# Column-tiled projections, spread Wo rows and DMA-transposed inputs in a recurrent attention kernel

## The chip, the cores and the metric

The kernel runs on one core of a Trainium2 chip. The metric is the device time of one execution in microseconds (us). A kernel's time is the median of its runs.

Names: PE is TensorE (PEld its weight loads), DVE is VectorE, ACT is ScalarE, POOL is GpSimd, SP is the engine that issues the DMAs.

## The reference, cut to what matters

```python
# S = 2048 rows, D = 512, 32 heads of 128, segments of 32 rows, 8 memory rows
mem = mem0
for s in range(64):                                # one segment after another
    h = concat([mem, x_ln[:, 32*s:32*s+32]])       # 8 memory rows + 32 rows of x
    q, k, v = h @ Wq, h @ Wk, h @ Wv               # 512 -> 32 heads x 128
    p = softmax(mask(q @ k.T * scale))
    o = (p @ v) @ Wo                               # 4096 -> 512
    mem = o[:, :8]                                 # goes into the next segment
    outs.append(o[:, 8:])
h = x + concat(outs)
# ... then a gMLP over h: gelu(LN(h) @ w_in), a 2048x2048 mix, w_out ...
```

The memory makes the 64 segments a chain. Of each segment's rows, 32 (8 memory rows and the first 24 rows of x) go through the chain. The last 8 rows of x are projected ahead, for 16 segments at once: that is the "X work" below. It does not depend on the chain, so the kernel uses it to fill PE's waits.

## The kernel before

A recorder collects operations for each engine, works out the semaphore waits, and emits everything unrolled. `pe(...)`, `dve(...)`, `act(...)`, `pool(...)`, `sp(...)` record one operation for that engine, and each engine runs its own in the recorded order.

The X work for Q and K: one 128x128 stationary block for each head and quarter of D, with 128 columns moving. One group is four heads, 16 matmuls:

```python
    def qkx_mm(ck, i, bank, hhs=range(4)):
        mi, h0 = i // 8, 4 * (i % 8)
        ws = (w_q, w_k)[mi]
        for hh in hhs:
            h = h0 + hh
            for dc in range(DC):                       # DC = 4
                pe(lambda e, h=h, dc=dc, hh=hh: e.matmul(ps[:, bank, hh * 128:(hh + 1) * 128],
                       lhsT=ws[:, dc, h * DH:(h + 1) * DH], rhs=hTe[:, ck % 3, dc, :],
                       start=(dc == 0), stop=(dc == DC - 1)), ...)
```

The chain's own projections, the Wo rows and the X work for V use four column tiles of 32: `tile_position=(0, 32 * c)`, output to 32 partitions. PV uses row tiles (`tile_position=(32 * c, 0)`). PV is the product p @ v, and its result is the context. Wo in the step is the context times Wo. F_group and WoX_scatter gather the finished output rows of a row block. An evacuation is a copy out of PSUM, where the matmuls write. One step, cut:

```python
    for s in range(NSEG):                              # NSEG = 64
        j4, rb = s % 4, s // 4                         # four steps are one row block of 128 rows
        # ... QK projections, mem_out(s - 1, 1), then `late` of the step before ...
        # ... S, exp, V, sums, ln, normalise (cut) ...
        xs = gx.pop(0) if gx else []                   # a V group in steps 0-15, a Q/K group in 16-47
        late = []
        for f in xs[:2]:                               # half of the X group
            f()
        PV_half(s, 0)
        PV_half(s, 1)
        for f in xs[2:4]:                              # the other half
            f()
        if j4 == 3 and rb > 0:
            F_group(rb - 1, WXB)
            WoX_scatter(rb - 1, WXB)
        # ... six context evacuations on ACT and DVE (cut) ...
        if j4 == 3 and rb > 0:
            F_add(rb - 1, WXB)
        Wo(WOQ, OB, 0, OC)
        # ... rest of Wo, part_evac, mem_out(s, 0): the memory rows for the next step (cut) ...
        if j4 == 3 and rb > 0:
            late.append(lambda rb=rb: h_done(rb - 1))
        late += xs[4:]                                 # the X group's evacuation, on DVE
        if j4 == 1 and 2 <= rb + 2 < RB:
            ln_inplace(0)                              # layernorm of a later x block, on DVE
        if j4 == 2 and 2 <= rb + 2 < RB:
            xT(0, FBK)                                 # four PE transposes
            late.append(lambda rb=rb: ring_copy(rb + 2, FBK))   # ACT
        if s + 1 < NSEG and s >= 3:
            WoX_mm((s + 1) // 4 - 1, (j4 + 1) % 4)     # batched Wo rows: 8 matmuls of 512 columns
        # ... loads, the evacuation of the Wo rows and the first steps' own cases (cut) ...
```

Of the kernel before, what the change touches and what calls it, by code (L numbers as in the profile page):

```python
# [169 lines left out]
def fast_path(nc, st, keep, A_x, A_mem0, A_Wq, A_Wk, A_Wv, A_Wo, A_seg_len, B_w_in, B_w_sp, B_b_sp, B_w_out, out):  # L170
# [82 lines left out]
    vext_d = nc.dram_tensor("vext_d", [NCK, 128, H * DH], BF, kind="Internal").ap()  # L253
    xn2_d = nc.dram_tensor("xn2_d", [RB, 128, D], BF, kind="Internal").ap()
    h_d = nc.dram_tensor("h_d", [RB, 128, D], BF, kind="Internal").ap()
    wT_d = nc.dram_tensor("wT_d", [S // 64, 128, RB, 64], BF, kind="Internal").ap()

    ps = st.enter_context(nc.psum_tensor("f_ps", [128, 8, 512], F32))
# [5 lines left out]
    def PB(b):  # L264
        return ("ps", b)
# [28 lines left out]
    def load_xe(ck, j):  # L294
        t, tok = xbuf(j)
        sp(lambda e: e.dma_start(t, xe[CK * ck:CK * ck + CK, XM:SEG, :]), writes=tok)
# [80 lines left out]
    def slot(s):  # L377
        return s % NSLOT

    def ring_copy(rb, bank):  # L380
        src = psb[:, bank, 0:512].rearrange("p (dc s c) -> p s dc c", dc=DC, s=4, c=SEG)[:, :, :, 0:XM]
        s0 = slot(4 * rb)
        act(lambda e: e.activation(out=hT[:, s0:s0 + 4, :, M:32], in_=src, func=ACT.Copy),
            reads=[PB(bank)], writes=[("hTx", rb % 3)])
# [14 lines left out]
# [5 lines that stand above are left out]
            for dc in range(DC):  # L404
                pe(lambda e, h=h, dc=dc, hh=hh: e.matmul(ps[:, bank, hh * 128:(hh + 1) * 128], lhsT=ws[:, dc, h * DH:(h + 1) * DH],  # L405
                                                         rhs=hTe[:, ck % 3, dc, :], start=(dc == 0), stop=(dc == DC - 1)),
                   reads=[("hTe", ck % 3), ("W", mi, h // 8)], writes=[PB(bank)])

    def qkx_evac(ck, i, bank, eng="act"):
        mi, h0 = i // 8, 4 * (i % 8)  # L410
        dst = QTx[ck % 2][:, mi, :, h0:h0 + 4, :].rearrange("p s h k -> p h s k")
        src = ps[:, bank, :].rearrange("p (h s k) -> p h s k", h=4, k=8)
        if eng == "act":
            act(lambda e: e.activation(out=dst, in_=src, func=ACT.Copy), reads=[PB(bank)], writes=[("QTx", ck % 2, mi, i % 8)])
        else:
            dve(lambda e: e.tensor_copy(out=dst, in_=src), reads=[PB(bank)], writes=[("QTx", ck % 2, mi, i % 8)])
# [76 lines left out]
    def qx_copy(s):  # L493
        j = s % CK
        buf = (s // CK) % 2
        dst = QT[:].rearrange("p b hp q r -> p (b hp) q r")[:, :, 0:8, :].rearrange("p hp q r -> p hp r q")
        src = QTx[buf][:, 0, j, :, :].rearrange("p (hp r) q -> p hp r q", r=2)
        pool(lambda e: e.tensor_copy(out=dst, in_=src), reads=[("QTx", buf, 0, i) for i in range(8)],
             writes=[("QTe", 0), ("QTe", 1)])
# [170 lines left out]
    def load_h(rb):  # L670
        sp(lambda e: e.dma_start(hbuf[:, rb % 2, :], xr[:, rb, :]), writes=[("h", rb % 2)])

    def WoX_mm(rb, qr):
        for bg in range(8):
            b, g = bg // 4, bg % 4
            h = 16 * b + 4 * qr + g
            pe(lambda e, h=h, g=g, i=8 * qr + bg: e.matmul(ps[32 * g:32 * g + 32, WXB, :], lhsT=cTx[:, rb % 2, i, :], rhs=w_o[:, h, :],  # L677
                                                           start=(i < 4), stop=(i >= H - 4), tile_position=(0, 32 * g)),
               reads=[("cTx", rb % 2), ("Wo", h // 8)], writes=[PB(WXB)])
# [4 lines left out]
    def WoX_scatter(rb, bank):  # L684
        for c in range(4):
            q = slice(32 * c, 32 * c + 32)
            pe(lambda e, q=q, c=c: e.matmul(ps[q, bank, :], lhsT=Sc[:, q], rhs=partx[:], start=False, stop=True, tile_position=(0, 32 * c)),
               reads=["partx", "Sc"], writes=[PB(bank)])
# [102 lines left out]
    gx = []  # L791

    def qkx_group(ck, i):
        gx.append([lambda hh=hh: qkx_mm(ck, i, XB, (hh,)) for hh in range(4)] + [lambda: qkx_evac(ck, i, XB, "dve")])

    def vx_group(ck, n):
        gx.append([lambda dc=dc: vx_mm(ck, n, XB, dc) for dc in range(DC)] + [lambda: vx_evac(ck, n, XB, "dve")])
# [21 lines left out]
               writes=[("wT", tb % 2, t)], after=after)  # L819

    lastop = {}
    qx_copy(0)
    for s in range(NSEG):
        j4 = s % 4
        rb = s // 4
        if j4 == 1 and rb > 0:
            load_h(rb - 1)
        if s == NSEG - 1:
            load_h(rb)
        if s % 2 == 1 and s // 2 < NWT:  # L830
            wT_piece(s // 2)
        if j4 == 0 and 2 <= rb + 2 < RB:
            load_x(rb + 2, 0)
        if s == 1:
            load_xe(3, 1)

        QK(s, QKP[0], (0, 1))
        if s > 0:
            mem_out(s - 1, 1)
            for f in late:  # L840
                f()
        QK(s, QKP[1], (0, 1))
        QK(s, QKP[0], (2, 3))
        QK_evac(QKP[0])
        QK(s, QKP[1], (2, 3))
        QK_evac(QKP[1])
        for piece in QKP[2:]:
            QK(s, piece)
            lastop["qk"[piece[3]]] = em.by_eng["pe"][-1]
            QK_evac(piece)  # L850
        if s == NSEG - 1:
            load_wT(0, [lastop["q"]])
        if s == 0:
            mask_pe()
        S_half(s, 0)
        sm_exp(0)
        V_half(s, 0, (0, 1, 2))
        sm_sums(0)
        sm_ln(0)
        S_half(s, 1)  # L860
        lastop["s"] = em.by_eng["pe"][-1]
        sm_exp(1)
        sm_rcp(0)
        V_half(s, 0, (3,))
        V_evac(0, "dve")
        if s == NSEG - 1:
            sp(lambda e: e.dma_start(w_in1, winr[:, :, 0:FH]), writes=["w_in1"], after=[lastop["s"], lastop["x"]])
            sp(lambda e: e.dma_start(bsp_b, bass.AP(B_b_sp.tensor, B_b_sp.offset, [[0, 128], [1, S]])), writes=["bsp"], after=[lastop["k"]])
            for r in range(8, RB - 2):
                xn2T_dma(r, [lastop["s"], lastop["x"]])  # L870
        V_half(s, 1, gs=(0, 2))
        sm_norm(0)
        V_evac(1, "dve", (0, 2))
        sm_sums(1)
        sm_ln(1)
        sm_rcp(1)
        V_half(s, 1, gs=(2, 4))
        lastop["v"] = em.by_eng["pe"][-1]
        V_evac(1, "act", (2, 4))
        sm_norm(1)  # L880
        if s + 1 < NSEG:
            qx_copy(s + 1)
            lastop["x"] = em.by_eng["pool"][-1]
            lastop["x"] = em.by_eng["pool"][-1]
        xs = gx.pop(0) if gx else []
        late = []
        for f in xs[:2]:
            f()
        PV_half(s, 0)
        PV_half(s, 1)  # L890
        for f in xs[2:4]:
            f()
        if j4 == 3 and rb > 0:
            F_group(rb - 1, WXB)
            WoX_scatter(rb - 1, WXB)
        cT_evac(0, "act", (0,))
        cT_evac(2, "dve", (0,))
        cT_evac(0, "act", (1,))
        cT_evac(2, "dve", (1,))
        cT_evac(1, "act")  # L900
        cT_evac(3, "dve")
        if j4 == 3 and rb > 0:
            F_add(rb - 1, WXB)
        Wo(WOQ, OB, 0, OC)
        part_evac(s, OB, 0, OC)
        Wo(WOQ[:6], OB2, OC, D)
        if s + 1 < NSEG:
            mem_out(s, 0)
            mask_dve()
        Wo(WOQ[6:], OB2, OC, D)  # L910
        cTx_copy(s)
        part_evac(s, OB2, OC, D)
        if j4 == 3 and rb > 0:
            late.append(lambda rb=rb: h_done(rb - 1))
        late += xs[4:]
        if j4 == 1 and 2 <= rb + 2 < RB:
            ln_inplace(0)
        if s == 3:
            ln_inplace(1)
        if j4 == 2 and 2 <= rb + 2 < RB:  # L920
            xT(0, FBK)
            late.append(lambda rb=rb: ring_copy(rb + 2, FBK))
        if s == 5:
            xT(1, FBK)
            late.append(lambda: xe_copy(3, FBK))
        if s + 1 < NSEG and s >= 3:
            WoX_mm((s + 1) // 4 - 1, (j4 + 1) % 4)
            if j4 == 2:
                late.append(lambda rb=rb: WoX_evac(rb - 1))
        if s + 1 == NSEG:  # L930
            for f in late:
                f()
        if s + 2 < NSEG:
            load_vx(s + 2)
        if j4 == 0 and rb >= 2:
            xn2_apply(rb - 2, rb % 2)
            xn2_store(rb - 2, rb % 2)
        if s == 3 * CK:
            free0 = [done47["s"], done47["x"]]
            sp(lambda e: e.dma_start(w_in2, winr[:, :, FH:F]), writes=["w_in2"], after=free0)  # L940
        if 0 <= s - 3 * CK - 1 < 8:
            xn2T_dma(s - 3 * CK - 1, free0)
        if s == 3 * CK - 1:
            done47 = {"s": lastop["s"], "x": px}
        px = lastop.get("x")
# [924 lines left out]
```

## Time and profile before

| | |
|---|---|
| time, median of 3 runs (4 with the one timed beside the change) | 902.19 us (902.04) |
| span of the profiled run | 903.8 us |
| to the first memory cast (prologue) | 69.3 us |
| V steps (memory casts 1 to 16) | 155.7 us |
| Q/K steps (16 to 48), 32 steps | 331.3 us, 10.35 us per step |
| last steps (48 to 63), without X work | 152.3 us |
| rest (last step, gMLP) | 195.2 us |

A step is measured from one "memory cast" to the next: the small DVE cast (128x16) that brings half of the new memory rows out of PSUM. The profile page first. Its lines are the span, PE's busy share, the busy share of 40 slices in tenths (PE, granted clock, DMA), the instruction queue (packets, MB, share), and the shares of the chain that ended last:

```profile
span 903.8 us, 48903 instructions
...
PE 870.1 (96%) x22506; PEld 537.7 (59%) x22513; DVE 499.6 (55%) x1231; ACT 451.9 (50%) x1274; POOL 156.4 (17%) x403
...
PE   7989999999999999999999999899999999999997
...
PEclk9999999999999999999999999999999999999999
DMA  9971211322203020312113120404123590022101
...
q8 instruction: 178, 2.92, 1.3%
...
PE 88%; DVE 7%; issue 2%; ACT 1%; POOL 1%; DMA 0%; SPq 0%; ACTq 0%
```

PE looks full. But matmuls overlap in these records, so "busy" says only that something was in flight.

The timeline of PE from V to Wo in a plain Q/K step (start, length, line, operation, tiles, count):

```profile
406.71 0.61 PE L573 MATMUL f_ps<-f_arena,f_hT 128*32 128x256 bf16 x16
407.26 0.62 PE L405 MATMUL f_ps<-f_hTe,f_arena 128*128 128x128 bf16 x8
407.81 0.27 PE L592 MATMUL f_ps<-f_E_sb,f_V_sb 32*128 32x40 bf16 x16
...
408.03 0.27 PE L592 MATMUL f_ps<-f_E_sb,f_V_sb 32*128 32x40 bf16 x16
...
408.34 0.62 PE L405 MATMUL f_ps<-f_hTe,f_arena 128*128 128x128 bf16 x8
408.89 0.84 PE L627 MATMUL f_ps<-f_arena,f_cT 128*32 128x256 bf16 x24
```

L573 is V, L405 the X work, L592 PV, L627 Wo. The X halves stand before and after PV, where PE would otherwise wait for the softmax and for the context evacuations. The last steps have no X work and take the same 9.95 us.

DVE at the start of a plain step, and of the step after the layernorm. The first stream transpose of Q starts 2.68 us after the memory cast of 400.76 in the first case, 3.45 us after that of 410.72 in the second, behind the layernorm (L353, L363) and the X cast (L416):

```profile
401.69 0.68 DVE L416 CAST f_arena<-f_ps 128x512 bf16<-128x512 f32 x1
403.44 0.45 DVE L491 STREAM_TRANSPOSE f_QT<-f_Tst 128x256 uint32<-128x256 uint32 x1 [1.06 <-ACT f_Tst L483]
...
411.34 0.69 DVE L353 BATCH_NORM_STATS2 f_st<-f_xn 128x6 f32<-128x512 bf16 x1
...
413.24 0.41 DVE L363 TENSOR_SCALAR f_xn<-f_xn,f_mv,f_rs 128x512 bf16<-128x512 bf16 x1 [1.00 <-POOL f_rs L357]
413.56 0.68 DVE L416 CAST f_arena<-f_ps 128x512 bf16<-128x512 f32 x1
414.17 0.43 DVE L491 STREAM_TRANSPOSE f_QT<-f_Tst 128x256 uint32<-128x256 uint32 x1
```

And the matmuls of the Q/K stage as groups (busy us, mean ns of one | idle time of PE just before them, in all):

```profile
L627 PE MATMUL f_ps<-f_arena,f_cT 128*32 128x256 bf16 x2056 | 64.8, 273 | 0.0
L405 PE MATMUL f_ps<-f_hTe,f_arena 128*128 128x128 bf16 x512 | 39.7, 221 | 0.0
```

### The profile page before, as it was taken

The numbers are of one execution on the slowest core, as the hardware profiler recorded it, in microseconds if no ns is written. First come the engines' busy times: TensorE is split into PE (matmuls) and PEld (weight loads), VectorE is DVE, ScalarE is ACT, GpSimd is POOL, SyncE is SP. The second block draws the span as 40 slices with busy tenths as digits, with TensorE's granted clock in tenths as the row PEclk, the third lists the DMA queues.
The fourth block names the chain that finished last, engine by engine and source line by source line (L and its number), as shares of the span: only waits on it lengthen the run. The fifth ranks groups of instructions, "written<-read, shape, count | busy, mean of one in ns | idle before, by whom it ended". The sixth has DMA issues, their size and how long they took to land.

```text
span 903.8 us, 48903 instructions
## 1 busy us (share of the span) xinstructions
PE 870.1 (96%) x22506; PEld 537.7 (59%) x22513; DVE 499.6 (55%) x1231; ACT 451.9 (50%) x1274; POOL 156.4 (17%) x403
## 2 busy tenths in 40 slices
PE   7989999999999999999999999899999999999997
PEld 6665666566666666666666666556566544434443
DVE  3435556566666656566666666555655554543343
ACT  2335566555566655666555666556665655300000
POOL 1501111121211211112212112111111122100000
PEclk9999999999999999999999999999999999999999
DMA  9971211322203020312113120404123590022101
GB/s 327 377 211 45 62 54 42 71 62 57 72 27 68 22 71 21 76 34 55 53 42 58 35 69 22 123 26 93 41 48 63 176 275 1 1 99 76 59 12 37
DMA packets 99586, 71.50 MB, mean 79 GB/s; under 512 B 62248, under 2 KB 84912, under 8 KB 99376
## 3 DMA queue, kind: packets, MB, share of 16 engines
q1 hardware_dynamic: 99376, 68.32, 27.6%
q8 instruction: 178, 2.92, 1.3%
q14 instruction: 32, 0.26, 0.1%
HBM read 39.46 MB, written 18.61 MB: 64 GB/s over the span
## 4 chain that ended last, share of the span: by engine, by line
PE 88%; DVE 7%; issue 2%; ACT 1%; POOL 1%; DMA 0%; SPq 0%; ACTq 0%
PE f_ps L472 21%; PE f_ps L627 13%; PE f_ps L573 11%; PE f_ps L1012 11%; PE f_ps L405 7%; PE f_ps L424 3%; PE f_ps L592 3%; PE f_ps L677 3%; PE f_ps L974 3%; PE f_ps L1005 3%; PE f_ps L1083 3%; PE f_ps L539 2%; DVE f_V_sb L584 2%; PE f_ps L598 1%; PE f_ps L519 1%
## 5 line engine op out<-in xcount | busy, mean ns | idle before, releaser
L472 PE MATMUL f_ps<-f_arena,f_hT 128*32 128x512 bf16 (+1 forms) x5120 | 239.9, 337 | 0.1
L472 PEld LDWEIGHTS f_ps<-f_arena,f_hT 128*32 128x32 bf16 x5120 | 125.8, 96 | 94.2 <-ACT f_hT L656 23.0
L483 ACT ACTIVATE f_Tst<-f_ps 128x512 bf16<-128x512 f32 (+1 forms) x320 | 148.5, 512 | 56.7 <-PE f_ps L472 47.1
L573 PE MATMUL f_ps<-f_arena,f_hT 128*32 128x256 bf16 (+1 forms) x3072 | 143.5, 308 | 0.5
L627 PE MATMUL f_ps<-f_arena,f_cT 128*32 128x256 bf16 x4096 | 133.5, 275 | 6.4 <-ACT f_cT L612 4.6
L563 POOL TENSOR_TENSOR f_E_sb<-f_R_sb,f_E_sb 128x64 bf16<-128x64 f32 x128 | 48.0, 375 | 409.3 <-ACT f_R_sb L555 409.3
L627 PEld LDWEIGHTS f_ps<-f_arena,f_cT 128*32 128x32 bf16 x4096 | 95.6, 96 | 29.2 <-ACT f_cT L612 11.5
L491 DVE STREAM_TRANSPOSE f_QT<-f_Tst 128x256 uint32<-128x256 uint32 x128 | 56.9, 445 | 89.5 <-ACT f_Tst L483 89.5
L1012 PE MATMUL f_ps<-f_arena 128*128 128x512 bf16 x448 | 103.0, 384 | 2.4 <-DVE f_arena L1018 1.6
L639 ACT ACTIVATE f_part<-f_ps 128x256 bf16<-128x256 f32 x128 | 49.0, 383 | 92.7 <-PE f_ps L627 92.7
L584 DVE TENSOR_SCALAR f_V_sb<-f_ps 128x512 bf16<-128x512 f32 (+1 forms) x128 | 70.6, 551 | 41.1 <-PE f_ps L573 41.1
L614 DVE TENSOR_SCALAR f_cT<-f_ps 128x160 bf16<-128x160 f32 (+1 forms) x192 | 61.0, 374 | 39.3 <-PE f_ps L598 39.3
L1012 PEld LDWEIGHTS f_ps<-f_arena 128*128 128x128 bf16 x448 | 43.9, 99 | 57.2 <-DVE f_arena L1018 2.6
L573 PEld LDWEIGHTS f_ps<-f_arena,f_hT 128*32 128x32 bf16 x3072 | 68.8, 96 | 14.5 <-ACT f_Tst L483 1.8
L612 ACT ACTIVATE f_cT<-f_ps 128x160 bf16<-128x160 f32 (+1 forms) x192 | 53.0, 349 | 40.0 <-PE f_ps L598 40.0
L405 PE MATMUL f_ps<-f_hTe,f_arena 128*128 128x128 bf16 x1024 | 70.4, 223 | 0.1
L491 DVE STREAM_TRANSPOSE f_KT<-f_Tst 128x128 uint32<-128x128 uint32 (+1 forms) x192 | 63.8, 338 | 3.1
L405 PEld LDWEIGHTS f_ps<-f_hTe,f_arena 128*128 128x128 bf16 x1024 | 58.9, 99 | 9.2 <-issue 7.1
L551 ACT ACTIVATE f_R_sb<-f_ps 128x160 f32<-128x160 f32 x128 | 38.8, 303 | 35.8 <-PE f_ps L544 35.8
L654 DVE CAST f_hT<-f_ps 128x16 bf16<-128x16 f32 x63 | 11.0, 175 | 78.2 <-PE f_ps L648 78.2
L1018 DVE TENSOR_TENSOR f_arena<-f_ps,f_arena 128x512 f32<-128x512 f32 x28 | 19.3, 691 | 59.5 <-PE f_ps L1012 59.5
L559 DVE TENSOR_TENSOR f_E_sb<-f_R_sb,f_E_sb 128x160 bf16<-128x160 f32 x128 | 45.6, 356 | 0.0
(103 smaller groups left out, 1089.5 us busy)
## 6 DMA issues: line engine op xcount, KB each, us to landing
wT_d<-f_wst SPq DMA_DIRECT2D x32, 256.0 KB, 2.5
f_arena<-wT_d SPq DMA_DIRECT2D x32, 256.0 KB, 4.3
f_arena<-in_A_Wq_dram SPq DMA_DIRECT2D x4, 1024.0 KB, 8.6
f_arena<-in_A_Wv_dram SPq DMA_DIRECT2D x4, 1024.0 KB, 14.3
f_arena<-in_A_Wk_dram SPq DMA_DIRECT2D x4, 1024.0 KB, 14.5
f_arena<-in_A_Wo_dram SPq DMA_DIRECT2D x4, 1024.0 KB, 8.5
f_Vx<-vext_d SPq DMA_DIRECT2D x64, 64.0 KB, 2.7
f_xn<-in_A_x_dram SPq DMA_DIRECT2D x17, 128.0 KB, 2.5
```

What stands on the lines that cost most here:

```text
L405: pe(lambda e, h=h, dc=dc, hh=hh: e.matmul(ps[:, bank, hh * 128:(hh + 1) * 128], lhsT=ws[:, dc, h * DH:(h + 1) * DH], rhs=hTe[:, ck % 3, d ...
L472: pe(lambda e, dc=dc, c=c, rhs=rhs: e.matmul(ps[32 * c:32 * c + 32, bank, 0:32 * nh], lhsT=hT[:, sl, dc, :], rhs=rhs, start=(dc == 0), sto ...
L483: act(lambda e: e.activation(out=st_.rearrange("p (hp i r) -> p hp i r", i=32, r=2), in_=ps[:, bank, 0:64 * np_].rearrange("p (hp r i) -> ...
L491: dve(lambda e: e.transpose(out=dst, in_=src), reads=tok, writes=[(nm, b, k) for k in halves(b, p0, np_)])
L563: pool(lambda e: e.tensor_tensor(out=ev, in0=rv, in1=ev, op=ALU.mult), reads=[("R", b), ("Ex", b)], writes=[("Ex", b)])
L573: pe(lambda e, dc=dc, c=c, c0=c0: e.matmul(ps[32 * c:32 * c + 32, bank, 0:w], lhsT=hT[:, sl, dc, :], rhs=w_v[:, dc, c0:c0 + w], start=(dc ...
L584: dve(lambda e: e.tensor_scalar(out=dst, in0=src, scalar1=VSC, scalar2=None, op0=ALU.mult), reads=[PB(bank)], writes=tok)
L612: act(lambda e: e.activation(out=dst, in_=src, func=ACT.Copy, scale=UNSC), reads=[PB(PVB[c])], writes=tok)
L614: dve(lambda e: e.tensor_scalar(out=dst, in0=src, scalar1=UNSC, scalar2=None, op0=ALU.mult), reads=[PB(PVB[c])], writes=tok)
L627: pe(lambda e, h=h, g=g, i=i, b=b, c=c: e.matmul(ps[32 * g:32 * g + 32, bank, 0:d1 - d0], lhsT=cTh[:, i, 8:40], rhs=w_o[:, h, d0:d1], star ...
L639: act(lambda e: e.activation(out=part[:, s % 8, d0:d1], in_=ps[:, bank, 0:d1 - d0], func=ACT.Copy), reads=[PB(bank)], writes=[("part", s % ...
L1012: pe(lambda e: e.matmul(ps[:, bank, 0:TB], lhsT=z2[:, sc, fb * 128:(fb + 1) * 128], rhs=wTb[tb % 2][:, :, sc, :], start=(sc == 0), stop=(s ...
```

## The change

Its intent: the same arithmetic in fewer PE mode changes and with less work on the chain.

- X work for Q/K in four column tiles of 32, as its neighbours V and Wo are. It can then follow V, and precede Wo, without a change of PE's tiling mode.
- Batched Wo rows in units of 4 matmuls, spread over the step's end and the wait before PV.
- x blocks transposed by DMA through a scratch tensor. Four PE transposes and an ACT copy go, and a DVE copy comes.
- DVE side work (layernorm, X evacuation) spread so that it does not delay the stream transposes.

The core of the diff:

```diff
+    def x_flip(j, i, dst, tok):
+        t, rd = xbuf(j)
+        sp(lambda e: e.dma_start(xs_d[i], t), reads=rd, writes=[("xs", i)])
+        sp(lambda e: e.dma_start_transpose(out=dst, in_=xs_d[i]), reads=[("xs", i)], writes=[tok])
...
+    def qkx_cols(ck, i, bank, hh):
+        mi, h = i // 8, 4 * (i % 8) + hh
+        ws = (w_q, w_k)[mi]
+        for dc in range(DC):
+            for c in range(4):
+                pe(lambda e, dc=dc, c=c: e.matmul(ps[32 * c:32 * c + 32, bank, hh * 128:(hh + 1) * 128],
+                                                  lhsT=ws[:, dc, h * DH + 32 * c:h * DH + 32 * c + 32], rhs=hTe[:, ck % 3, dc, :],
+                                                  start=(dc == 0), stop=(dc == DC - 1), tile_position=(0, 32 * c)),
...
     def qkx_group(ck, i):
-        gx.append([lambda hh=hh: qkx_mm(ck, i, XB, (hh,)) for hh in range(4)] + [lambda: qkx_evac(ck, i, XB, "dve")])
+        gx.append([lambda hh=hh: qkx_cols(ck, i, XB, hh) for hh in range(4)] + [lambda: qkx_evac(ck, i, XB, "dve")])
...
-        for f in xs[:2]:
-            f()
-        PV_half(s, 0)
-        PV_half(s, 1)
-        for f in xs[2:4]:
-            f()
+        nw1, nw4 = ((1, 1, 1, 0)[j4], (2, 2, 0, 1)[j4]) if s < 3 * CK else (3, 0)
         if j4 == 3 and rb > 0:
             F_group(rb - 1, WXB)
             WoX_scatter(rb - 1, WXB)
+        xs = gx.pop(0) if gx else []
+        fill = xs[:4]
+        if j4 == 3 and s < 3 * CK:
+            fill = xs[1:4]
+        for f in fill[:-2]:
+            f()
+        for f in wq[:nw1]:
+            f()
+        del wq[:nw1]
+        PV_half(s, 0)
+        PV_half(s, 1)
+        for f in fill[-2:]:
+            f()
...
+            late += xs[4:]                             # step 3 of a row block
+        else:
+            for f in xs[4:]:                           # the X evacuation, now before Wo
+                f()
...
-        if j4 == 2 and 2 <= rb + 2 < RB:
-            xT(0, FBK)
-            late.append(lambda rb=rb: ring_copy(rb + 2, FBK))
+        if j4 == 0 and 2 <= rb + 2 < RB:
+            late.append(lambda: ln_stats(0))
+        if j4 == 0 and 2 <= rb + 1 < RB:
+            late.append(lambda rb=rb: ring_fill(rb + 1))
...
+            if j4 == 3:
+                wq.extend(lambda rb=rb, k=k: WoX_mm(rb, k // 2, range(4 * (k % 2), 4 * (k % 2) + 4)) for k in range(8))
+            elif j4 == 2 and gx:
+                gx[0][0]()
+            for f in wq[:nw4]:
+                f()
```

More of the change, by code (lines that the diff above doesn't have):

```diff
@@ L255, in fast_path @@
     h_d = nc.dram_tensor("h_d", [RB, 128, D], BF, kind="Internal").ap()
+    xs_d = nc.dram_tensor("xs_d", [RB + 1, 128, D], BF, kind="Internal").ap()
     wT_d = nc.dram_tensor("wT_d", [S // 64, 128, RB, 64], BF, kind="Internal").ap()
@@ L378, in slot, with ring_fill @@
         return s % NSLOT
+    def x_flip(j, i, dst, tok):
+        t, rd = xbuf(j)
+        sp(lambda e: e.dma_start(xs_d[i], t), reads=rd, writes=[("xs", i)])
+        sp(lambda e: e.dma_start_transpose(out=dst, in_=xs_d[i]), reads=[("xs", i)], writes=[tok])
+    def ring_fill(rb):
+        src = xn[:, 1, :].rearrange("p (dc s c) -> p s dc c", dc=DC, s=4, c=SEG)[:, :, :, 0:XM]
+        s0 = slot(4 * rb)
+        dve(lambda e: e.tensor_copy(out=hT[:, s0:s0 + 4, :, M:32], in_=src), reads=[("xn", 1)], writes=[("hTx", rb % 3)])
     def ring_copy(rb, bank):
@@ L406, in qkx_mm @@
                                                          rhs=hTe[:, ck % 3, dc, :], start=(dc == 0), stop=(dc == DC - 1)),
+                   reads=[("hTe", ck % 3), ("W", mi, h // 8)], writes=[PB(bank)])
+    def qkx_cols(ck, i, bank, hh):
[6 more added lines that the diff above has]
+                                                  start=(dc == 0), stop=(dc == DC - 1), tile_position=(0, 32 * c)),
                    reads=[("hTe", ck % 3), ("W", mi, h // 8)], writes=[PB(bank)])
@@ L671, in load_h, with WoX_mm @@
         sp(lambda e: e.dma_start(hbuf[:, rb % 2, :], xr[:, rb, :]), writes=[("h", rb % 2)])
-    def WoX_mm(rb, qr):
-        for bg in range(8):
+    def WoX_mm(rb, qr, bgs=range(8)):
+        for bg in bgs:
             b, g = bg // 4, bg % 4
@@ L821, in fast_path @@
     lastop = {}
+    wq = []
     qx_copy(0)
@@ L834, in fast_path @@
         if s == 1:
-            load_xe(3, 1)
+            load_xe(3, 7)
         QK(s, QKP[0], (0, 1))
@@ L884, in fast_path @@
             lastop["x"] = em.by_eng["pool"][-1]
-        xs = gx.pop(0) if gx else []
         late = []
-        for f in xs[:2]:
-            f()
-        PV_half(s, 0)
-        PV_half(s, 1)
-        for f in xs[2:4]:
-            f()
+        nw1, nw4 = ((1, 1, 1, 0)[j4], (2, 2, 0, 1)[j4]) if s < 3 * CK else (3, 0)
         if j4 == 3 and rb > 0:
@@ L903, in fast_path @@
             F_add(rb - 1, WXB)
+            late += xs[4:]
+            late.append(lambda rb=rb: h_done(rb - 1))
+        else:
+            for f in xs[4:]:
+                f()
         Wo(WOQ, OB, 0, OC)
@@ L912, in fast_path @@
         part_evac(s, OB2, OC, D)
-        if j4 == 3 and rb > 0:
-            late.append(lambda rb=rb: h_done(rb - 1))
-        late += xs[4:]
+        if j4 == 0 and 2 <= rb + 2 < RB:
+            late.append(lambda: ln_stats(0))
+        if j4 == 0 and 2 <= rb + 1 < RB:
+            late.append(lambda rb=rb: ring_fill(rb + 1))
         if j4 == 1 and 2 <= rb + 2 < RB:
-            ln_inplace(0)
+            late.append(lambda rb=rb: (ln_apply(0), x_flip(0, rb, xn[:, 1, :].rearrange("p (dc c) -> p dc c", dc=DC), ("xn", 1))))
+        if s == 2:
+            late.append(lambda: ln_stats(7))
         if s == 3:
-            ln_inplace(1)
-        if j4 == 2 and 2 <= rb + 2 < RB:
-            xT(0, FBK)
-            late.append(lambda rb=rb: ring_copy(rb + 2, FBK))
-        if s == 5:
-            xT(1, FBK)
-            late.append(lambda: xe_copy(3, FBK))
-        if s + 1 < NSEG and s >= 3:
-            WoX_mm((s + 1) // 4 - 1, (j4 + 1) % 4)
-            if j4 == 2:
-                late.append(lambda rb=rb: WoX_evac(rb - 1))
-        if s + 1 == NSEG:
+            late.append(lambda: (ln_apply(7), x_flip(7, RB, hTe[:, 0, :, :], ("hTe", 0))))
+        if j4 == 1 and rb >= 2:
+            late.append(lambda rb=rb: (xn2_apply(rb - 2, rb % 2), xn2_store(rb - 2, rb % 2)))
+        if j4 == 2 and rb > 0:
+            assert not wq
+            late.append(lambda rb=rb: WoX_evac(rb - 1))
+        if s + 1 < NSEG:
+            if j4 == 3:
[4 more added lines that the diff above has]
+                f()
+            del wq[:nw4]
+        else:
             for f in late:
@@ L934, in fast_path @@
             load_vx(s + 2)
-        if j4 == 0 and rb >= 2:
-            xn2_apply(rb - 2, rb % 2)
-            xn2_store(rb - 2, rb % 2)
         if s == 3 * CK:
```

## The prediction

> **What bounds it now.** 64 recurrent steps fill 60 to 709 us of the 904. From one memory evacuation (the 128x16 VectorE cast) to the next, the timeline gives 9.95 us for a plain step, the same in the last sixteen steps, which have no X projection. So a plain step is bound by a latency chain (normalise, PV, context evacuation, Wo, memory) that X work only fills: the memory cast follows the first context evacuation by 2.28 us, with X or without. The rest is excess: where Q/K are projected four steps take about 41.3 us, not 39.8. The step after the layernorm takes 10.48 and the one after the x transpose 10.84 us.
>
> **Terms, per four steps (estimates from the timeline).**
> 1. The 10.48 us step: bn_stats 0.69, aggregate 0.18, apply 0.41 us and the X cast 0.68 us queue on VectorE before the Q/K stream transposes, which start 0.8 us late. The diff spreads these and puts the cast behind the context evacuations, where VectorE idles 1.26 us. Gain 0.5 us.
> 2. The 10.84 us step: four PE transposes (0.33 us in the chain) and the 0.48 us ScalarE ring copy go; F_group and scatter (0.43 us, then after PV) move ahead of PV, into the wait for the softmax. Gain 0.8 us.
> 3. Fewer Wo rows at the step's end (8 matmuls, 0.43 us): Q/K starts 0.23 instead of 0.43 us after the memory cast, as in the first steps, which have none. But there only 0.12 us of it reached the end of V. Two of four steps get it, all of the last sixteen. Gain 0.2 to 0.4 us, 0.5 to 0.8 at the end.
> 4. Cost: X half 0.44 plus one 4-matmul Wo unit 0.21 us before PV is 0.65 us, against a natural wait of 0.7 us to PV's second half: PV, and all after it, comes about 0.08 us later, 0.3 us per row block.
> 5. Column tiles for X: the 128x128 matmuls already run at 55 ns for 128 columns, so four column tiles at best tie. What goes are mode changes: 0.10 us before the X half and 0.09 us after the second. The Trainium skill (TensorEngine Tiling (Array Packing), Key Properties) says a change of tiling mode drains TensorE; the trace agrees (0.21 us from V's last matmul to X's first, where 0.11 is the pace). But they lie in slack: I count zero.
>
> Sum: 1.35 us per row block over twelve blocks, 0.8 over the last four: 16 + 3, about 19 us, plus 1 us from the first block. Prologue and gMLP tail unchanged.
>
> **Predicted: 882 us, range 870 to 893.** Faster by over 2%: 0.58; within 2%: 0.40; slower: 0.02.
>
> **Right or wrong shows in:** step lengths of a row block becoming nearly equal (9.85 to 10.05 us); stream transposes 2.5 to 2.7 us after the memory cast in every step; no PE transposes or ring copies in the loop; PV 0.1 us later; column-tiled X at about 14 ns per matmul.
>
> **What would make it wrong.** Column-tiled X issues four times the instructions: if PE is fed too slowly, or weight loads show, each 10 ns per matmul costs 0.6 us per step, 20 us in all. DMA: storing and DMA-transposing x can starve instruction fetch (a 1.4 us "issue" gap at 575 us, while w_in loads) or hold the in-order DMA queue ahead of the Vx loads. Better: if the earlier Q/K reaches each step's end whole, 8 us more.

## More of the kernel before

The busy times in the three stages of the loop come next (V, Q/K and last steps; counts of instructions in brackets):

```profile
core 0: us, PE busy (x) PEld busy (x) DVE busy (x) ACT busy (x) POOL busy (x), PEclk, DMA share, GB/s
69.30:225.00 155.70, 154.26 (x4952) 96.77 (x4948) 94.58 (x250) 93.33 (x278) 29.88 (x74) 1.00 0.21 56
225.00:556.30 331.30, 329.44 (x10600) 219.06 (x10592) 204.40 (x536) 198.99 (x592) 64.42 (x160) 1.00 0.21 49
556.30:708.60 152.30, 142.96 (x4724) 91.19 (x4717) 85.68 (x233) 92.75 (x275) 29.02 (x72) 1.00 0.28 63
```

Two quotients of the Q/K row matter later: 10600 + 10592 PE instructions in 32 steps are 662 per step, and in 331.3 us they are 64.0 per us.

## The result, and the profile after

The changed kernel takes 928.18 us (926.22 to 930.87, 4 runs) against 902.04 us: slower. The ratio is 1.0284 (95% interval 1.0246 to 1.0322). Ratios here are the mean time of one kernel's runs over that of the other's of the same rounds, so not quite the ratio of the medians. Executions over 1.5% slower than the fastest of the same kernel are left out of the means.

The same lines of the page, after:

```profile
span 924.4 us, 51906 instructions
...
PE 856.3 (93%) x23982; PEld 528.2 (57%) x23989; DVE 504.6 (55%) x1245; ACT 449.8 (49%) x1259; POOL 157.1 (17%) x403
...
PE   6999999999998899898988998999999999999997
...
PEclk9999999999999999999999999999999999999999
DMA  9953223234212212222221212332412392021201
...
q8 instruction: 190, 3.11, 1.4%
...
PE 91%; issue 5%; DVE 2%; ACT 1%; DMA 1%; SPq 0%; POOL 0%
```

"Issue", time in which the engine waited for nothing that the profile shows, went from 2% of the chain to 5%. The stages:

```profile
core 0: us, PE busy (x) PEld busy (x) DVE busy (x) ACT busy (x) POOL busy (x), PEclk, DMA share, GB/s
66.40:219.00 152.60, 149.37 (x4928) 91.98 (x4924) 95.31 (x251) 92.46 (x273) 30.00 (x74) 1.00 0.32 71
219.00:581.90 362.90, 325.50 (x12107) 220.34 (x12098) 207.29 (x544) 198.00 (x584) 64.80 (x160) 1.00 0.23 51
581.90:731.00 149.10, 140.87 (x4720) 86.09 (x4709) 86.42 (x236) 92.41 (x273) 29.09 (x72) 1.00 0.28 67
```

The V steps gained 3.1 us and the last steps 3.2 us. The Q/K steps lost 31.6 us: from 10.35 to 11.34 us per step, irregular, between 10.5 and 12.5. PE is *less* busy there (325.5 of 362.9 us, before 329.4 of 331.3). The groups of that stage:

```profile
L648 PE MATMUL f_ps<-f_arena,f_cT 128*32 128x256 bf16 x2056 | 70.8, 273 | 19.6 <-issue 18.5 <-ACT f_cT L633 1.1
L425 PE MATMUL f_ps<-f_hTe,f_arena 128*32 128x128 bf16 x2048 | 43.8, 220 | 9.6 <-issue 9.5
```

L648 is Wo and L425 the column-tiled X work. PE idled 28 us of "issue" before these two groups alone. PE's timeline shows how:

```profile
307.22 1.47 PE L648 MATMUL f_ps<-f_arena,f_cT 128*32 128x256 bf16 x43
309.80 0.40 PE L648 MATMUL f_ps<-f_arena,f_cT 128*32 128x256 bf16 x8 [1.12 <-issue]
...
316.71 0.62 PE L425 MATMUL f_ps<-f_hTe,f_arena 128*32 128x128 bf16 x31
318.21 0.23 PE L425 MATMUL f_ps<-f_hTe,f_arena 128*32 128x128 bf16 x1 [0.88 <-issue]
```

The stop is in the middle of a group. The first 31 matmuls of an X half run at 56 ns for each four (14.0 ns per matmul, as predicted). Then the 32nd, which waits for no semaphore, comes 1.1 us after the one before it.

What had been meant for DVE did work. The statistics (L354) and the ring copy (L389) now stand one step earlier in the row block than the old layernorm did. That step starts the first stream transpose 2.68 us after the memory cast, and so does the next one, which was the late one before (3.45 us), where no stall intervenes:

```profile
503.71 0.18 DVE L675 CAST f_hT<-f_ps 128x16 bf16<-128x16 f32 x1 [2.12 <-PE f_ps L669]
...
504.32 0.69 DVE L354 BATCH_NORM_STATS2 f_st<-f_xn 128x6 f32<-128x512 bf16 x1
...
505.14 0.23 DVE L389 COPY f_hT<-f_xn 128x384 bf16<-128x384 bf16 x1
506.39 0.45 DVE L512 STREAM_TRANSPOSE f_QT<-f_Tst 128x256 uint32<-128x256 uint32 x1 [1.02 <-ACT f_Tst L504]
```

**The theory (A).** PE is starved of instructions. Every matmul is two PE instructions, a weight load and a matmul, so 48 more matmuls per Q/K step are 96 more instructions: 756 to 758 instead of 662. (The count moves by two with where the window is cut.) In the changed kernel they run at 24205 / 362.9 us = 66.7 per us. Three observations point at the supply. In the 0.40 us of that X half PE starts 31 matmuls, 78 per us, where the mean of the stage is 33, so it is not slow at each instruction. The instruction queue moves packets of 16384 bytes: 12 packets more for 3003 more instructions, so about 250 instructions each. And in the Q/K stage such a packet starts every 3.8 us, while the gaps above end 1.4 to 1.6 us after a packet has landed (packets started at 307.50 and 314.98 us and took 0.95 and 1.64; the gaps ended at 309.80 and 318.21).

**Rivals.** B: the added DMA store and transpose of x slow the fetch. C: the new order of work makes the stalls. D: 32-column weight loads or matmuls are slow in PE itself.

### The profile page after: what moved, and what is told of

Same layout as the page of the kernel before. It is cut to its first block, busy times and chain, and to the rows that moved or that the text cites. A ratio compares the mean times of both kernels' runs of the same rounds, so it can differ in the third digit from the quotient of the medians.

```text
span 924.4 us, 51906 instructions
## 1 busy us (share of the span) xinstructions
PE 856.3 (93%) x23982; PEld 528.2 (57%) x23989; DVE 504.6 (55%) x1245; ACT 449.8 (49%) x1259; POOL 157.1 (17%) x403
## 4 chain that ended last, share of the span: by engine, by line
PE 91%; issue 5%; DVE 2%; ACT 1%; DMA 1%; SPq 0%; POOL 0%
PE f_ps L493 25%; PE f_ps L648 13%; PE f_ps L594 12%; PE f_ps L1049 10%; PE f_ps L425 4%; PE f_ps L416 3%; PE f_ps L445 3%; PE f_ps L698 3%; PE f_ps L1011 3%; PE f_ps L1042 3%; PE f_ps L613 2%; PE f_ps L1120 2%; PE f_ps L560 2%; PE f_ps L540 1%; PE f_ps L619 1%
## 5 line engine op out<-in xcount | busy, mean ns | idle before, releaser
L648 PE MATMUL f_ps<-f_arena,f_cT 128*32 128x256 bf16 x4096 | 138.3, 273 | 27.7 <-issue 20.4
L648 PEld LDWEIGHTS f_ps<-f_arena,f_cT 128*32 128x32 bf16 x4096 | 96.2, 95 | 51.5 <-issue 25.0
L512 DVE STREAM_TRANSPOSE f_KT<-f_Tst 128x128 uint32<-128x128 uint32 (+1 forms) x192 | 65.8, 343 | 4.7 <-ACT f_Tst L504 0.8
L425 PE MATMUL f_ps<-f_hTe,f_arena 128*32 128x128 bf16 x2048 | 43.8, 220 | 9.6 <-issue 9.5
L437 DVE CAST f_arena<-f_ps 128x512 bf16<-128x512 f32 x48 | 32.9, 685 | 23.9 <-PE f_ps L416 21.0
```

Of the source, the lines that this page charges most:

```text
L425: pe(lambda e, dc=dc, c=c: e.matmul(ps[32 * c:32 * c + 32, bank, hh * 128:(hh + 1) * 128], lhsT=ws[:, dc, h * DH + 32 * c:h * DH + 32 * c ...
L512: dve(lambda e: e.transpose(out=dst, in_=src), reads=tok, writes=[(nm, b, k) for k in halves(b, p0, np_)])
L648: pe(lambda e, h=h, g=g, i=i, b=b, c=c: e.matmul(ps[32 * g:32 * g + 32, bank, 0:d1 - d0], lhsT=cTh[:, i, 8:40], rhs=w_o[:, h, d0:d1], star ...
```

## The experiments

### The change with wide X work

```diff
     def qkx_group(ck, i):
-        gx.append([lambda hh=hh: qkx_cols(ck, i, XB, hh) for hh in range(4)] + ...
+        gx.append([lambda hh=hh: qkx_mm(ck, i, XB, (hh,)) for hh in range(4)] + ...
```

> The whole change, but the Q/K part of X stays one 128x128 matmul per block instead of four 128x32 ones. Theory A (PE is starved of instructions: in the changed kernel 758 PE instructions per Q/K step run at 66.8 per us, steps of 11.36 us): with 662 per step supply no longer binds, Q/K steps fall to 9.8 to 9.9 us, total 876 to 886 us. Rival B (the added DMA store and transpose of x slow the fetch of instructions): steps stay above 11 us, total 922 to 932. Rival C (the new order of work itself makes the stalls): as B.

Measured: 891.06 us (889.56 to 893.74), ratio to before 0.9885 (0.9839 to 0.9930). Q/K steps of 10.24 us. The "issue" time before Wo and X in the Q/K stage is gone (first the stage, then the two groups):

```profile
217.20:544.80 327.60, 326.69 (x10571) 212.26 (x10560) 206.71 (x545) 197.75 (x584) 64.40 (x160) 1.00 0.24 56
...
L648 PE MATMUL f_ps<-f_arena,f_cT 128*32 128x256 bf16 x2055 | 66.5, 273 | 0.6 <-issue 0.5
L416 PE MATMUL f_ps<-f_hTe,f_arena 128*128 128x128 bf16 x512 | 41.1, 221 | 0.0
```

With the DMA transposes and the new order still in, B and C are out as the main cause. The total is 5 us above the range given: the steps did not reach 9.9 us. That is taken up below.

### Column tiles alone, in the kernel before

The kernel before, with `qkx_cols` added and used in `qkx_group`, and nothing else.

> The kernel before with only the Q/K part of X in four column tiles. Theory A: 758 instructions per Q/K step at 66.8 per us is 11.35 us where before had 10.35; 32 steps, so about 934 us (925 to 940). Rivals B and C: within 5 us of before (898 to 907), as neither the DMA nor the order changed.

Measured: 934.89 us (930.66 to 938.09), ratio 1.0349 (1.0296 to 1.0401). Q/K steps of 11.36 us, at (12140 + 12132) / 363.5 us = 66.8 instructions per us. A different order and no added DMA, and the same rate:

```profile
L637 PE MATMUL f_ps<-f_arena,f_cT 128*32 128x256 bf16 x2056 | 69.4, 273 | 10.4 <-issue 10.4
L414 PE MATMUL f_ps<-f_hTe,f_arena 128*32 128x128 bf16 x2048 | 42.4, 220 | 9.1 <-issue 9.1
```

So the column tiles suffice for the loss. What remains is whether it is their count or their kind.

### The count without the tiles: 48 useless matmuls

To the wide-X kernel, 48 matmuls of 8 columns per Q/K step are added. Later matmuls overwrite what they write, so the result is right.

```diff
+    def tiny(bank):
+        for k in range(24):
+            c = k % 4
+            pe(lambda e, c=c: e.matmul(ps[32 * c:32 * c + 32, bank, 0:8], lhsT=ident[:, 32 * c:32 * c + 32], rhs=ident[:, 0:8],
+                                       start=True, stop=True, skip_group_check=True, tile_position=(0, 32 * c)), ...)
...
+        if CK <= s < 3 * CK:
+            tiny(OB)                        # and tiny(XB) before the first X quarter
         Wo(WOQ, OB, 0, OC)
```

> As the wide-X run, plus 48 useless 8-column matmuls in each Q/K step (24 before the first X half, 24 before Wo), whose results are overwritten: the instruction count of the column-tiled X without its tiles. Theory A: about the time of the changed kernel, Q/K steps 11.3 to 11.5 us, 922 to 935 us. Rival D (column-tiled X is slow in the array or in its weight loads, not in its supply): the tiny matmuls take at most 0.3 us of array time per step, so at most 10 us above the wide-X run, 876 to 896 us.

Measured: 930.71 us (929.34 to 931.51), ratio 1.0317 (1.0274 to 1.0361). Q/K steps of 11.35 us, at 66.7 instructions per us. The X work is wide here, and "issue" time stands before Wo (L655) and before the tiny matmuls (L433):

```profile
217.40:580.50 363.10, 341.83 (x12108) 234.21 (x12100) 206.79 (x545) 197.94 (x584) 64.57 (x160) 1.00 0.22 51
...
L655 PE MATMUL f_ps<-f_arena,f_cT 128*32 128x256 bf16 x2056 | 68.5, 272 | 8.8 <-issue 8.7
...
L433 PE MATMUL f_ps<-f_ident 128*32 128x8 bf16 x1536 | 21.4, 168 | 4.7 <-issue 4.7
```

D falls. Where nothing stops them, the 24 tiny matmuls of a group start within 0.15 us, so the two groups take 0.3 us of a step, and the step grew by 1.1 us. The loss comes with the number of instructions. One limit stays: the tiny matmuls are column tiles with 32-column weights themselves, and no run here adds instructions of the wide form.

### Two column tiles

`qkx_cols` with two tiles of 64 columns instead of four of 32, otherwise the whole change.

> The whole change with the Q/K part of X in two column tiles of 64: 694 PE instructions per Q/K step. Theory A: 694 at 66.8 per us is 10.4 us per step, about 17 us above the wide-X run, 892 to 903 us. Rivals B and C: 922 to 932. Rival D: no number, somewhere between the wide-X run and the changed kernel.

Measured: 901.91 us (899.67 to 903.35), ratio 0.9990 (0.9947 to 1.0033). Q/K steps of 10.49 us, 692 instructions per step, 66.0 per us. A's range and, within 0.1 us, its step held: 26 of the 37 us between the changed kernel and the wide-X run came back for two thirds of the extra instructions taken away. (The "17 us above the wide-X run" in the same expectation does not fit its own 10.4 us, which over 10.24 us is 5 us in 32 steps; 10.9 us were measured.) At this dose the whole change is worth nothing.

### One block of wide X work

The first attempt to beat both kernels. From the wide-X kernel, in the Q/K steps only: all X quarters before PV, two Wo units (or F_group and scatter) after it, and one unit at the step's end in two of four steps.

```diff
-        for f in fill[:-2]:
+        for f in (fill if one else fill[:-2]):
             f()
...
         PV_half(s, 1)
-        for f in fill[-2:]:
-            f()
+        if one:
+            if j4 == 3:
+                F_group(rb - 1, WXB)
+                WoX_scatter(rb - 1, WXB)
+            else:
+                for f in wq[:2]:
+                    f()
+                del wq[:2]
```

> As the wide-X run, but in the Q/K steps all four wide X quarters stand in one block before PV (two mode changes instead of four) and two batched Wo units or F_group stand after PV. If mode changes are what keeps the wide-X run's Q/K steps at 10.24 us where the V steps reach 9.8 to 10.0: Q/K steps about 10.0 us, 5 to 8 us below the wide-X run, 883 to 887 us. If not (supply, or the later PV, keeps them there): 888 us or more.

Measured: 894.72 us (893.06 to 897.90), ratio 0.9884 (0.9842 to 0.9925); before took 906.39 us on this chip. A miss: not distinguishable from the wide-X kernel. The usual step did fall, to 10.12 us, but the mean was 10.30 us because some steps stalled for 0.1 to 1.4 us. The step just after these 32, the first of the last sixteen, took 12.85 us.

### Less other DMA traffic

The changed kernel with its column tiles, but without the w_sp transposes and stores in the Q/K steps (they are done two at a time in the other steps):

```diff
-        if s % 2 == 1 and s // 2 < NWT:
-            wT_piece(s // 2)
+        if s % 2 == 1 and not CK <= s < 3 * CK:
+            k = s // 2 if s < CK else s // 2 - 16
+            wT_piece(2 * k)
+            wT_piece(2 * k + 1)
```

> The changed kernel, column tiles kept, with the w_sp DMA transposes and stores taken out of the Q/K steps (done twice as often in the others). If other DMA traffic sets the time of an instruction block (3.83 us for 256 now): intervals of the instruction queue fall, Q/K steps under 11 us, total under 918. If the turnaround is the fetch's own: Q/K steps stay at 11.2 to 11.4, total 922 to 932.

Measured: 930.75 us (925.23 to 936.94), ratio 1.0275 (1.0207 to 1.0343). The Q/K stage:

```profile
220.50:586.00 365.50, 325.51 (x12107) 220.87 (x12100) 207.17 (x544) 197.91 (x584) 64.54 (x160) 1.00 0.12 30
```

The DMA share fell from 0.23 to 0.12 and the traffic from 51 to 30 GB/s, but the steps stayed at 11.42 us and the rate at 66.2 per us. The packets of the instruction queue started every 3.86 us in the mean, in the changed kernel every 3.83. This traffic does not set the rate.

### Fewer instructions, column tiles kept

The changed kernel, in the Q/K steps with the second half of V as 16 matmuls of 512 columns instead of 32 of 256:

```diff
-        V_half(s, 1, gs=(0, 2))
+        V_half(s, 1, (0, 1), gs=(0, 4))
         sm_norm(0)
-        V_evac(1, "dve", (0, 2))
         sm_sums(1)
         sm_ln(1)
         sm_rcp(1)
-        V_half(s, 1, gs=(2, 4))
-        V_evac(1, "act", (2, 4))
+        V_half(s, 1, (2, 3), gs=(0, 4))
+        V_evac(1, "act", (0, 4))
```

> The changed kernel, column tiles kept, with the second half of V in the Q/K steps as 16 matmuls of 512 columns, not 32 of 256: 726 PE instructions per step instead of 758, with a V evacuation that comes later. Theory A: 726 at 66.8 per us is 10.87 us, about 16 us less in all, 908 to 917 us. If what counts is the column tiling of X (rival D): no gain, or some us slower through the later evacuation, 926 to 936.

Measured: 917.63 us (913.28 to 923.92), ratio 1.0157 (1.0103 to 1.0211); by the 2% verdict unclear against before. Q/K steps of 10.99 us, 724 instructions each, 65.9 per us:

```profile
218.50:570.10 351.60, 329.74 (x11596) 211.07 (x11588) 197.35 (x513) 204.64 (x584) 64.41 (x160) 1.00 0.24 53
```

Some 10 us came back by removing 32 instructions per step that have nothing to do with X. The direction is A's; the step is 0.1 us longer than A's number, and the time lies just above A's range.

### Wo rows at the end of the step again

```diff
-        nw1, nw4 = ((1, 1, 1, 0)[j4], (2, 2, 0, 1)[j4]) if s < 3 * CK else (3, 0)
+        nw1, nw4 = 0, 2
```

This is from the wide-X kernel.

> The wide-X run with the batched Wo rows all at the end of the steps again (8 matmuls each, as before the change). My terms 3 and 4: in the last sixteen steps 9.95 instead of 9.77 us (3 us in all); in the X steps the earlier PV and the later Q/K cancel, within 0.1 us per step. Total 2 to 7 us above the wide-X run, 893 to 898. If spreading the rows is the main gain: above 899.

Measured: 894.05 us (892.50 to 895.66), ratio 0.9876 (0.9839 to 0.9912), with before at 906.39 us on this chip. The absolute time lies in the range, but by the ratio (0.9885 for the wide-X kernel) there is no difference in the whole. Step by step it went as the terms say. The last sixteen steps are mostly 9.95 us instead of 9.77. In the Q/K steps two of four are shorter (9.96 instead of 10.2) and the one with F_group is longer (10.50 instead of 10.08). So by the lengths of the plain steps, spreading the Wo rows gains about 3 us in the last steps, and nothing that these runs can show in the X steps. (The sums of the last stage do not show it: they also hold a stop at the load of w_in, of which more below.)

### One block of X and the merged V

Both edits above in one kernel: 628 PE instructions per Q/K step.

> A version meant to beat both: the one-block run (wide X, two mode changes) with the merged V half of the Q/K steps: 630 PE instructions per Q/K step, well under the supply. If the stalls left in the one-block run (steps of 10.12 us, but 10.30 in the mean) come from supply too, the mean falls to 10.12 to 10.18 us: 4 to 6 us less, ratio to before 0.980 to 0.985. If they come from elsewhere: ratio 0.986 to 0.992.

Measured: 889.40 us (885.27 to 891.64, 6 runs), ratio 0.9854 (0.9821 to 0.9887). The Q/K stage of the profile:

```profile
215.00:539.60 324.60, 323.10 (x10060) 191.41 (x10052) 197.06 (x513) 204.67 (x584) 64.65 (x160) 1.00 0.24 56
```

Of the 32 steps 27 take 10.11 to 10.13 us and the other five 10.15 to 10.60. The step just after them took 12.65 us. The steps fell as expected for a supply with room. The ratio falls just outside the first range and just below the second.

### The wide-X kernel again, on that chip

> The wide-X run again, on the chip of the run above: ratio to before 0.984 to 0.992.

Measured: 891.01 us (888.19 to 893.83, 6 runs), ratio 0.9861 (0.9826 to 0.9897). The kernel with one block and merged V is not distinguishable from it in time (0.9854), though its Q/K steps are steadier.

### Twice the dose

96 useless matmuls per Q/K step instead of 48.

> The wide-X run with 96 useless 8-column matmuls per Q/K step, twice the earlier dose: 854 PE instructions. Theory A: 854 at 66.8 per us is 12.8 us per Q/K step, about 975 us in all (965 to 985). If something other than the count had made the earlier dose slow: below 955.

Measured once, state unknown: 981.41 us, Q/K steps of 12.98 us, 852 instructions each, 65.7 per us. As A said.

```profile
216.80:632.20 415.40, 361.26 (x13643) 251.71 (x13632) 207.06 (x544) 198.06 (x584) 64.67 (x160) 0.99 0.20 46
```

### All doses together

From the stage tables of the profiles, Q/K steps only, in the order of the instruction count:

| kernel | X work | PE instructions per step | us per step | per us |
|---|---|---|---|---|
| one block, merged V | wide | 628 | 10.14 | 62.0 |
| wide X | wide | 660 | 10.24 | 64.5 |
| before | wide | 662 | 10.35 | 64.0 |
| two tiles | 2 tiles | 692 | 10.49 | 66.0 |
| merged V | 4 tiles | 724 | 10.99 | 65.9 |
| the change | 4 tiles | 756 | 11.34 | 66.7 |
| quiet DMA | 4 tiles | 756 | 11.42 | 66.2 |
| 48 tiny | wide | 757 | 11.35 | 66.7 |
| tiles alone | 4 tiles | 759 | 11.36 | 66.8 |
| 96 tiny | wide | 852 | 12.98 | 65.7 |

The three kernels left out (one block, Wo rows at the end, wide X again) have 660 instructions and take 10.20 to 10.30 us. From some 690 instructions per step on, the mean rate stands at 66 to 67 per us and the step's length follows the count. Below that it does not.

The packed traces show where PE stops (this is counted from their records). In the Q/K stage of the changed kernel there are 41 stretches of more than 0.5 us in which no PE instruction starts, 46.5 us in all. Number the PE instructions in order of their starts: from each stop to the next it is a whole multiple of 255.3 instructions, one to three times, with an error of less than one instruction. Each stop ends 1.0 to 1.6 us after a packet of the instruction queue has landed. The 34 stops of the tiles alone, the 29 of 48 tiny, the 25 of the merged V and the 58 of 96 tiny lie and end in the same way (multiples of 255.3 to 255.4 with an error of up to 1.2 instructions, 1.2 to 1.7 us); in the wide-X kernel there are 2. So PE stops at the border of a block of instructions and waits for a packet. A limit on PE's own pace would not choose these places.

## Why the prediction was wrong

The step that failed is the fifth term: "Column tiles for X ... four column tiles at best tie ... I count zero." It costs 35 us: the Q/K stage takes 362.9 us with the column tiles and 327.6 us with wide X in the otherwise equal kernel. The array time of the tiles was right (14.0 ns per matmul). What was missing from the sum is a resource that I had only listed as a risk, the supply of instructions. In the mean of the Q/K stage PE got at most 66 to 67 per us in any kernel here, that is 256 in 3.8 us, and the kernel before already used 64.0. The change asked for 756 per step; in the 9.9 us that I expected of a step, that would have been 76 per us. Dividing the two counts of the stage table by its length shows the demand before anything is built. Only the ceiling is not in that trace, though the 1.4 us "issue" gap that I had seen there should have made me look for it: it ended at 575.97 us, 1.4 us after a packet had landed, as the stops in the changed kernel do.

The page that I had at hand points the other way. The Trainium skill, Runtime: NRT & Kernel Launch, Instruction fetch mechanics, says that instructions come in blocks of 16 KiB (256 instructions) while the current one executes, and that the cost of a block boundary is "mostly hidden". The block size agrees (16384 bytes per packet, about 250 instructions). "Hidden" does not, at these rates: an X half stopped after its 31st matmul for 1.1 us.

The other terms, in the Q/K steps read from the kernels with wide X:

1. The step after the layernorm: right in kind. The stream transposes start 2.68 us after the memory cast (before 3.45), and the step went from 10.48 to 10.22 us. I had counted 0.5 us.
2. The step after the x transpose: right. From 10.84 to 10.08 us, with 0.8 us predicted.
3. Fewer Wo rows at the step's end: right, and better in the last sixteen steps. A plain step there takes 9.77 instead of 9.95 us, so the earlier Q/K reached the end of the step whole. I had allowed for 0.12 of 0.2 us.
4. The cost of the Wo unit before PV was mis-sized for wide X. In the second step of a row block PV starts 7.38 us after the memory cast instead of 7.05, and plain Q/K steps take 10.2 instead of 9.96 us. Where X is column-tiled and PE was not starved, PV started at 7.15 (0.1 later, as predicted), and its last matmul came at 7.45 as before.

So wide X before PV costs 0.2 us there where tiled X does not, in the same order of work. That fits mode changes, whose hiding wait is now used by the Wo unit, but no run takes the mode changes away alone. With one block of X (two mode changes less, but X and Wo rows moved as well) the usual step is 10.12 instead of 10.2 us.

Of the 20 us that I expected, the wide-X kernel has 10 to 13 (ratios 0.9885 and 0.9861). The V and last stages together gave 8 us in its profile (151.1 + 148.7 us against 155.7 + 152.3), close to the 9 that the terms imply for them. The Q/K stage gave 3.7 us instead of 11. (In the profile of its repetition it was 5 and 5 us, with one step of 13.25 us at the load of w_in.) The supply caps it as well: 660 instructions at 66.7 per us are 9.9 us, an estimate of the shortest mean step, so the 9.85 us steps that I had named could not be had on average.

What stays open: what in the fetch takes 3.8 us for a block, of which the packet itself takes 1.1 us (median in the changed kernel). It is not the traffic of the w_sp transposes, and the mix of instructions that was tried did not matter. Other traffic may delay a block. In nine of the 13 profiles two packets started 6.2 to 7.4 us apart around the load of w_in, and PE stood still for 1.5 to 3.2 us just after (in the last version 6.6 and 1.7 us). In the other four the packets stayed under 5.6 us apart and PE stood still there for 0.7 to 1.5 us. No run takes the load away, so its part is not shown. The stalls of 0.1 to 1.4 us in single steps of the wide-X kernels became rarer with 628 instructions per step. Those in one stretch of over 0.5 us, 14 in the profiles of the five wide-X kernels, also end 1.3 to 1.5 us after a packet; for the shorter ones the cause was not settled.

## What to carry to other kernels

Count the instructions of an engine per stage and divide by the stage's time before splitting matmuls into tiles. On PE every matmul counts twice, and in this kernel the supply ended at a mean of 66 to 67 per us, in every mix of instructions that was tried. A change that is neutral in the array can cost 35 us if it multiplies instructions where that rate is nearly used up. "Issue" gaps in the middle of a group, ending 1.0 to 1.7 us after a packet of the instruction queue has landed, and lying multiples of 255 instructions apart, are its mark in these traces.

## What the Trainium skill lacked or had wrong

- Runtime: NRT & Kernel Launch, Instruction fetch mechanics: calls the cost of a 16 KiB block boundary mostly hidden. Here PE got no more than 66 to 67 instructions per us over 32 steps (256 in 3.8 us), stood still for about 1.1 us at a time, and the Q/K stage lost 35 us to it. The page gives no rate of supply. It says only that blocks fill faster than instructions are dispatched, and PE's stops at the block borders show that this did not hold here.
- TensorEngine Tiling (Array Packing), Performance Considerations: names about 60 cycles per matmul as the instruction overhead and the copy out of PSUM as what may become the bottleneck. Column tiles of 128 columns ran here at 14.0 ns per matmul, and the bottleneck was the number of instructions. Four column tiles multiply those of X by four (from 660 to 756 per step in all). The page does not mention it.
- TensorE: Matmul & The Clock Gate, Part 1: says that start-to-start never drops below about 25 ns. In column tiles the matmuls of one set of four started 3 to 4 ns apart, and sets of 40-column matmuls (PV, in row tiles) followed each other at 25 ns per four. The floor holds here per set of four tiles, not per matmul. Part 3 of the same page has about 4 ns between the starts of tiles, which agrees, so only Part 1, read alone, is wrong.
